# Attention and a routed MoE layer on one core: when queries and keys are loaded, and for how many units at once

## The chip, the core and the metric

One core of one Trainium2 chip runs the whole program in one launch. The metric is the device time of one execution in microseconds (us). The cores' engines are called as the profile calls them: PE (matrix products, with PEld for its weight loads), DVE, ACT and POOL (elementwise work), and SP, which here does nothing but issue DMAs.

## What is computed

For 8 batches and 12 heads, with 448 tokens and a head dimension of 64:

```python
q_n, k_n = (rmsnorm(q, g_q), rmsnorm(k, g_k))
scores = scale * np.matmul(q_n, k_n.transpose(0, 1, 3, 2))
attn = softmax(scores)                       # row maximum taken off, 1e-9 added to the sum
x = np.matmul(attn, v)                       # then as 3584 tokens of 12 * 64 = 768
e_idx = np.argmax(x @ w_gate + modality_bias[modality_id], axis=1)
out[mask] = gate_w[mask, None] * (np.maximum(x[mask] @ w1[e], 0.0) @ w2[e])   # for each of 8 experts
```

All in float32. The products run in PE's fp32r format with a high and a low part of each operand, so that one product takes three passes, or two where parts are stacked.

## The kernel before

**Units and steps.** A unit is two heads of one batch: 48 units. Attention is laid out by hand over steps n, from -22 (`PLAN['start']`) to 335. Unit u's scores are taken in the seven steps 7u to 7u+6, one block of 128 score rows a step (`st`, L974), beside preparatory work for later units and the rest of the work for earlier ones. `plan` says what each step does; `when(what, u)` gives the step, `7u - PLAN[what]`, unless `PLAN['first']` names another for one of the first units. All engines run under a manual schedule, so the order of the program is the order on each engine and on each DMA queue. The routed layer follows from about 580 us on, and the change does not touch it.

**A unit's way.** Its queries and keys are loaded (`load`, the DMA at L794) as [112 partitions, 2 heads, 4 x 64]; squared on ACT (`sumsq`: queries at step 7u-50, keys at 7u-49), summed, turned into a reciprocal root (`rstd`), and scaled on POOL (`norm`, steps 7u-26, queries, then keys). PE transposes them (`tr`, L869: keys at 7u-21, queries at 7u-18), and a step later ACT and DVE split the result into a high and a low part. The parts then have to change partitions, and SP moves them within on-chip memory by DMA (`move`, L882, 112 KB each): in step 7u-20 four moves for the keys (two high, two low), in step 7u-17 four for the queries. The row maximum's products (`sa`, L946) begin at step 7u-14 and read both. `mt` brings the maxima into a row of the queries' tile by a small DMA (L962). Values are loaded at the end of each seventh step (`load_v`, L787), and every third unit's results are stored (`xstore`, L1086).

**The loads' buffers.** There are six slots for queries (`r1[0]`) and six for keys (`r1[1]`), slot u mod 6. A load therefore waits until unit u-6's `norm` has read its slot; a load for two units at once waits for units u-6 and u-5. One `load(u, n, which)` issues one DMA each for queries (0) and keys (1), over n units: 224 KB for one unit, 448 KB for two.

**When they are issued.** Ahead of the steps: units 0 and 1 singly, 2 and 3 together, the gains `g_q` and `g_k`, units 4 and 5 together. At the end of step -12 units 6 and 7 together, keys first. Units 8 and 9 singly at the ends of steps -2 (`7u - PLAN['ld']`, with `ld` 58) and 6. From unit 10 on, for two units at once, keys at the end of step 7u-57 and queries at the end of step 7u-54. Within a step the transposes' moves come first, the loads last.

**SP's queue.** SP issues one DMA after another. Each carries its own wait, so whatever stands behind a waiting DMA waits too.

Of the kernel before, what the change touches and what calls it, by code (L numbers as in the profile page):

```python
# [66 lines left out]
def kernel(  # L67
# [59 lines left out]
    def load_gains():  # L127
        with nc.allow_non_contiguous_dma(reason="gains, one to a partition"):
            for half in range(2):
                SY.dma_start(gg[64 * half : 64 * half + 64, 0:1], g_q.unsqueeze(1))  # L130
                SY.dma_start(gg[64 * half : 64 * half + 64, 1:2], g_k.unsqueeze(1))
# [261 lines left out]
    def view(t, off, p, *dims):  # L393
        n = 1
        for d in dims:
            n *= d
        a = t[:p, off : off + n]
        if len(dims) > 1:
            ax = " ".join("abcd"[: len(dims)])
            a = a.rearrange(f"p ({ax}) -> p {ax}", **dict(zip("abcd"[1:], dims[1:])))  # L400
        return a
# [367 lines left out]
    if True:  # L769
# [19 lines left out]
        def load(u, n=1, which=(0, 1)):  # L789
            b, h0 = u // NP, 2 * (u % NP)  # L790
            for g in which:
                for m in range(n):
                    T.setdefault(u + m, {})["qk"[g]] = ld_b[g][(u + m) % 6]
                SY.dma_start(view(r1[g], QK * (u % 6), CP, 2 * n, NCH * D),  # L794
                             (q, k)[g][b, h0 : h0 + 2 * n].rearrange("h (p c) d -> p h (c d)", p=CP))
# [428 lines left out]

        wps = ps_o.tile([128, 512], F32, tag="o", name="warm")
        A.preload_act_table_set("natural_log_exp_and_others")
        for u, n in ((0, 1), (1, 1), (2, 2)):
            load(u, n)
        load_gains()
        load(4, 2)  # L1230

        pre = {e: {} for e in "AV"}
        post, fin = {}, {}
# [21 lines left out]
        def put(n, *what):  # L1255
            plan.setdefault(n, []).append(what)
# [10 lines left out]
        def xt_at(u):  # L1267
            if u < NU - 8:
                return NJ * (u + 6) + XTJ
            return NJ * (NU - 2 + (u - NU + 8) // 2) + XTE[u % 2]  # L1270

        def when(what, u):
            return P["first"].get((what, u), NJ * u - P[what])

        for u in range(NU):
            for j in range(NJ):
                jj = (0, 1, 2, 4, 5, 6, 3)[j] if u < P["early"] else j
                put(when("sa", u) + j * (P["sastep"] if u == 0 else 1), "sa", u, jj)
            put(when("mt", u), "mt", u)
            if u < NU - 1:  # L1280
                for c in range(4):
                    put(NJ * (u + 1) + (AVJ[c] if u < NU - 2 else min(AVJ[c], 6)), "av", u, c)
            put(xt_at(u), "xt", u)
            if u % 2:
                put(NJ * (u + 1) + (SMJ if u < NP * (B - 2) else P["sml"]), "sums", u - 1)
            if u % 4 == 3:
                put(NJ * (u + 2) + (LAJ if u < NP * (B - 2) else min(LAJ, 4)), "gates", u // 4)
                put(NJ * (u + 2) + (RCJ if u < NP * (B - 2) else min(RCJ, 6)), "recips", u // 4)
            put(when("tk", u), "tr", u, 1)
            put(when("tq", u), "tr", u, 0)  # L1290
            put(when("nq", u), "norm", u, 0)
            put(when("nk", u), "norm", u, 1)
            put(when("sk", u), "sq", u, 1)
            put(when("sq", u), "sq", u, 0)
            if ("rs", u) in P["first"]:
                put(when("rs", u), "rs", u // 3, P["rs0"].get(u, 0), u % 3 + 1)
            elif u > 8 and u % 3 == 2:
                put(when("rs", u), "rs", u // 3, 0, 3)
            if u == 6:
                put(-12, "load", u, 2, (1, 0))  # L1300
            elif u in (8, 9):
                put(when("ld", u), "load", u)
            elif u > 9 and u % 2 == 0:
                put(when("ld", u) + 1, "load", u, 2, (1,))
                put(when("ld", u) + 4, "load", u, 2, (0,))

        for n in range(P["start"], NJ * NU):
            i, j = divmod(n, NJ)
# [127 lines left out]
        u, g = NU - 1, NU // 4 - 1  # L1436
# [182 lines left out]
```

## Time and profile before

| | |
|---|---|
| median of three runs | 1083.87 us (1081.62 to 1086.3) |
| the profiled execution | 1088.99 us |
| its span, first to last instruction | 1087.2 us |
| busy share of the span | PE 96%, DVE 72%, POOL 65%, ACT 64% |
| mean granted clock of PE | 0.986 |
| DMA of the span | 153.72 MB, mean 141 GB/s |

A busy PE means that some product is under way, not that it runs at its peak. The granted clock is the share of PE's full clock, 1.0 (2.4 GHz) or 0.5 (1.2 GHz); a stretch that holds both shows a mean between them. An idle time in brackets in a timeline names what is believed to have ended it.

### The profile page before, as it was taken

The page shows a single profiled execution, that of the slowest core. Times are in us where ns is not written, and L with a number is a line of the kernel's source. Part 1 is how long each engine was busy: PE and PEld are TensorE (multiplying, and loading weights), DVE is VectorE, ACT ScalarE, POOL GpSimd, SP SyncE. Part 2 cuts the span into 40 slices and gives each one's busy share as a digit, 9 for nine tenths or more (in the row PEclk, how much of TensorE's full clock was granted, in tenths as well). Part 3 has the DMA queues.
Part 4 walks back from the last instruction along what each step waited for, and adds up shares of the span by engine and source line. Part 5 has one row for each costly group of instructions (what it writes and reads, how often), then busy time and mean ns, then how long its engine had stood idle before and what let it go on. Part 6 is the DMA issues. An engine that isn't in the chain of part 4 may idle for free.

```text
span 1087.2 us, 18988 instructions
## 1 busy us (share of the span) xinstructions
PE 1047.1 (96%) x6536; PEld 808.6 (74%) x6536; DVE 782.4 (72%) x1351; ACT 696.1 (64%) x1293; POOL 704.7 (65%) x728
## 2 busy tenths in 40 slices
PE   8899999989999999999999999999999999999996
PEld 7645555545555555555556999999999999999995
DVE  5676778968779887798878897667655676566740
ACT  6787888868888787786665555555545555455531
POOL 6787777777876878688776566664455544656451
PEclk9899999989999999999999999999999999999998
DMA  7775767757876669673684822533284422244161
GB/s 177 173 179 123 167 161 170 176 122 163 169 163 165 154 168 165 151 166 90 131 263 132 219 61 78 155 119 93 55 289 147 117 85 67 84 117 117 46 219 61
DMA packets 151704, 153.72 MB, mean 141 GB/s; under 512 B 73434, under 2 KB 141486, under 8 KB 151088
## 3 DMA queue, kind: packets, MB, share of 16 engines
q1 hardware_dynamic: 126244, 110.59, 42.7%
q0 software_dynamic: 25328, 41.82, 12.4%
q8 instruction: 54, 0.88, 0.4%
q14 instruction: 50, 0.41, 0.2%
q10 hardware_dynamic: 28, 0.01, 0.0%
HBM read 150.31 MB, written 33.39 MB: 169 GB/s over the span
## 4 chain that ended last, share of the span: by engine, by line
PE 74%; DMA 8%; DVE 6%; issue 5%; POOL 4%; ACT 2%; SPq 0%; POOLq 0%; DVEq 0%; ACTq 0%
PE ph L565 19%; PE py L595 18%; PE av L1013 11%; PE st L974 11%; DMA w1w<-xw 5%; PE sa L946 4%; PE tr L869 3%; PE xt L1070 2%; DVE at_hlw L52 2%; POOL r2w L52 1%; PE sm L1028 1%; POOL xrw L52 1%; PE warm L1223 1%; ACT xw L52 1%; DVE xw L52 1%
## 5 line engine op out<-in xcount | busy, mean ns | idle before, releaser
L565 PE MATMUL ph<-xw,w1w 128*128 128x256 f32 x2016 | 246.6, 283 | 1.4 <-DVE xw L52 0.8
L565 PEld LDWEIGHTS ph<-xw,w1w 128*128 128x128 f32 x2016 | 244.0, 192 | 3.8 <-issue 1.4
L52 DVE TENSOR_REDUCE at_hlw<-sa 128x1 f32<-128x448 f32 x336 | 205.7, 617 | 42.8 <-PE sa L946 24.4
L974 PE MATMUL st<-w1w 128*128 128x448 f32 (+1 forms) x480 | 177.1, 418 | 0.8 <-DMA w1w<-xw 0.6
L946 PE MATMUL sa<-w1w 128*128 128x448 f32 (+1 forms) x288 | 112.2, 390 | 20.0 <-ACT w1w L52 5.8
L52 POOL TENSOR_TENSOR r2w<-r2w 128x448 f32<-128x448 f32 (+1 forms) x72 | 82.1, 1140 | 64.4 <-DVE r2w L52 23.8
L52 ACT ACTIVATE r2w<-st 128x448 f32<-128x448 f32 x168 | 90.7, 543 | 48.5 <-PE st L974 40.6
L974 PEld LDWEIGHTS st<-w1w 128*128 128x128 f32 (+1 forms) x480 | 85.4, 191 | 45.4 <-ACT r2w L52 15.6
L52 POOL DMA_INDIRECT r<-in_moe_w_dram,tb_w x60 | 78.1, 1301 | 57.8 <-DVE w1w L52 42.5
L595 PE MATMUL py<-w2lw,hhw 128*128 128x384 f32 x448 | 113.7, 334 | 0.0
L52 ACT ACTIVATE hhw<-ph 128x512 fp32r<-128x512 f32 x56 | 33.5, 598 | 120.9 <-PE ph L565 102.0
L52 DVE TENSOR_TENSOR w1w<-r,w1w 128x768 fp32r<-128x768 f32 x112 | 103.4, 953 | 8.9 <-ACT w1w L52 7.3
L52 ACT CAST w1w<-xw 64x448 fp32r<-64x448 f32 x188 | 105.5, 561 | 3.4 <-issue 1.4
L52 POOL DMA_INDIRECT r2w<-in_moe_w_dram,tb_vi x48 | 51.0, 1062 | 86.3 <-DVE w2lw L52 73.7
L52 DVE TENSOR_TENSOR w2lw<-r2w,w2ha 128x1536 fp32r<-128x1536 f32 x28 | 49.1, 1757 | 79.2 <-issue 50.3
L52 ACT ACTIVATE at_w2lw<-st 128x448 f32<-128x448 f32 x168 | 90.5, 544 | 22.6 <-PE st L974 17.5
L974 PE MATMUL st<-w1w,w2ha 65*128 65x448 f32 x288 | 101.1, 371 | 1.1 <-DMA w1w<-xw 1.1
L52 POOL TENSOR_TENSOR xrw<-r,at_hlw 112x512 f32<-112x512 f32 x95 | 98.0, 1051 | 5.0 <-PE tr L869 4.5
L52 ACT CAST w1w<-r 128x768 fp32r<-128x768 f32 x112 | 95.0, 901 | 0.0
L946 PEld LDWEIGHTS sa<-w1w 128*128 128x128 f32 (+1 forms) x288 | 55.8, 194 | 35.1 <-issue 10.5
L52 POOL TENSOR_TENSOR r2w<-r2w,at_w2lw 64x448 f32<-64x448 f32 (+1 forms) x48 | 54.7, 1140 | 41.8 <-DVE r2w L52 18.1
L595 PEld LDWEIGHTS py<-w2lw,hhw 128*128 128x128 f32 x448 | 80.9, 188 | 0.0
(313 smaller groups left out, 2208.5 us busy)
## 6 DMA issues: line engine op xcount, KB each, us to landing
w1w<-xw SPq DMA_DIRECT2D x312, 112.0 KB
xg<-xrw SPq DMA_DIRECT2D x14, 768.0 KB
xrw<-xg SPq DMA_DIRECT2D x56, 192.0 KB
r<-in_q_dram SPq DMA_DIRECT2D x22, 448.0 KB
r<-in_k_dram SPq DMA_DIRECT2D x22, 448.0 KB
w2ha<-xw SPq DMA_DIRECT2D x72, 112.0 KB
r2w<-in_v_dram SPq DMA_DIRECT2D x24, 224.0 KB
at_w2lw<-in_v_dram SPq DMA_DIRECT2D x24, 224.0 KB
```

The source lines that it names most:

```text
L52: return fn(*a, **kw)
L565: PE.matmul(ps[:, i], lhsT=lt_, rhs=rt_[:, c], start=n == 0, stop=n == 17)
L595: PE.matmul(ps[n][:, :384], lhsT=lt_[:, j, 128 * t : 128 * t + 128], rhs=rt_[:, 384 * n : 384 * n + 384], start=j == 0 and m == 0, stop=j ...
L869: PE.transpose(sp[:, c], src[:, c], idn[:CP, :CP])
L946: PE.matmul(ps[:, :S], lhsT=t["qq"][r, h, a : a + 128], rhs=t["kk"][h][r], start=True, stop=True)
L974: PE.matmul(ps[:, :S], lhsT=l, rhs=t["qq"][:, h] if first else t["ql"][:, h], start=first and (j != 3 or h == 0), stop=not first and (j != ...
L1013: PE.matmul(t["av"][64 * h : 64 * h + 64, :S], lhsT=vv[r, u % 3, j], rhs=t["p"][r, j], start=c == 0, stop=c == 3)
L1028: PE.matmul(R[g][32 * i : 32 * i + 32, :S], lhsT=sel[:, m], rhs=T[u + i // 2]["cs"][:, i % 2], start=m == 0, stop=False, tile_position=(0, ...
L1070: PE.transpose(ps[:CP, 128 * c : 128 * c + 128], T[u]["xt"][:, c * CP : (c + 1) * CP], idn)
L1223: PE.matmul(wps[:, :128], lhsT=ones, rhs=idn, start=True, stop=True)
```

## The change

The program's first six units are loaded singly instead of one, one, two and two; so are units 6 and 7, by the plain formula (steps -16 and -9); units 8 and 9 stay as they were. From unit 10 on the loads are still for two units at once. The keys stay at step 7u-57. The queries move from step 7u-54 to step 7u-59, ahead of the keys.

```diff
-        for u, n in ((0, 1), (1, 1), (2, 2)):
-            load(u, n)
+        for u in range(3):
+            load(u)
         load_gains()
-        load(4, 2)
+        for u in range(3, 6):
+            load(u)
...
-            if u == 6:
-                put(-12, "load", u, 2, (1, 0))
-            elif u in (8, 9):
+            if 5 < u < 10:
                 put(when("ld", u), "load", u)
             elif u > 9 and u % 2 == 0:
+                put(when("ld", u) - 1, "load", u, 2, (0,))
                 put(when("ld", u) + 1, "load", u, 2, (1,))
-                put(when("ld", u) + 4, "load", u, 2, (0,))
```

## Rows read from the trace of the kernel before

**Rows 1.** Stretches of four units: us, PE, PEld, DVE, ACT, POOL busy (count), clock, DMA share, GB/s

```profile
134.80:178.60 43.80, 43.80 (x242) 25.47 (x240) 35.98 (x67) 36.18 (x80) 31.86 (x33) 1.00 0.74 178
...
222.80:274.30 51.50, 47.18 (x243) 26.73 (x241) 39.45 (x78) 37.11 (x80) 36.49 (x38) 0.93 0.66 153
...
410.10:458.00 47.90, 45.60 (x243) 26.37 (x241) 35.64 (x67) 36.18 (x80) 35.26 (x36) 0.96 0.81 164
```

**Rows 2.** Waits of PE, 100 to 480 us: total us, times, longest

```profile
PE sa L946 <- issue: 4.7, 2, 4.3
PE sa L946 <- DMA w1w<-xw: 4.3, 4, 2.3
```

**Rows 3.** Timeline of PE: the three longest of these waits (start, us, ...)

```profile
227.95 0.71 PE L946 MATMUL sa<-w1w 128*128 128x448 f32 x1 [4.32 <-issue]
...
320.74 0.44 PE L946 MATMUL sa<-w1w 128*128 128x448 f32 x1 [0.89 <-DMA w1w<-xw]
...
435.42 0.71 PE L946 MATMUL sa<-w1w 128*128 128x448 f32 x1 [2.30 <-DMA w1w<-xw]
```

**Rows 4.** Timeline of SP's queue ahead of the wait at 320 us

```profile
304.10 2.42 SPq L882 DMA_DIRECT2D w1w<-xw  x4
...
307.33 0.60 SPq L794 DMA_DIRECT2D r<-in_k_dram  x1
307.99 1.89 SPq L787 DMA_DIRECT2D r2w<-in_v_dram  x1
310.07 2.61 SPq L882 DMA_DIRECT2D w1w<-xw  x4
...
313.64 0.42 SPq L794 DMA_DIRECT2D r<-in_q_dram  x1
315.16 2.52 SPq L882 DMA_DIRECT2D w1w<-xw  x4
```

**Rows 5.** Chain of waits, two moves: start, us from issue to landing

```profile
34.14 2.02 DMA w1w<-xw
...
315.16 5.45 DMA w1w<-xw
```

**Rows 6.** Timeline of SP's queue and of ACT around the wait at 223 us

```profile
219.63 0.42 SPq L794 DMA_DIRECT2D r<-in_q_dram  x1
220.16 2.44 SPq L882 DMA_DIRECT2D w1w<-xw  x4
...
227.34 0.63 ACT L52 ACTIVATE xrw<-r 112x512 f32<-112x512 f32 x1 [4.67 <-DMA r<-in_q_dram]
```

**Rows 7.** Timeline of PE, of SP and chain of waits at step -5

```profile
30.06 0.71 PE L946 MATMUL sa<-w1w 128*128 128x448 f32 x1 [3.40 <-ACT w1w L52]
...
24.52 2.38 SPq L882 DMA_DIRECT2D w1w<-xw  x4
...
23.94 4.74 DMA r<-in_q_dram
```

**Rows 8.** Stretches of the start, columns as in rows 1

```profile
2.00:12.00 10.00, 10.00 (x78) 9.98 (x76) 3.89 (x11) 4.23 (x9) 6.18 (x13) 1.00 0.97 243
12.00:26.66 14.66, 11.96 (x66) 9.12 (x64) 10.21 (x18) 11.92 (x27) 10.66 (x23) 0.88 0.62 152
26.66:30.06 3.40, 0.00 (x1) 0.03 (x1) 0.00 (x0) 1.79 (x4) 2.25 (x10) 0.87 1.09 241
30.06:34.80 4.74, 4.74 (x19) 4.53 (x20) 2.53 (x5) 1.19 (x4) 2.09 (x3) 0.50 0.89 152
```

**Rows 9.** Timeline of DVE (the gains' product) and of POOL (unit 3's norm)

```profile
11.75 0.16 DVE L52 TENSOR_TENSOR gs<-gg 128x1 f32<-128x1 f32 x1 [1.83 <-DMA gg<-in_g_k_dram]
...
30.18 2.04 POOL L52 TENSOR_TENSOR xrw<-r,at_hlw 112x512 f32<-112x512 f32 x2
```

**Rows 10.** Timeline of SP (a single unit's load) and of POOL (two norms)

```profile
1.73 0.46 SPq L794 DMA_DIRECT2D r<-in_q_dram  x1
...
300.86 2.04 POOL L52 TENSOR_TENSOR xrw<-r,at_hlw 112x512 f32<-112x512 f32 x2
```

## Prediction

> **What bounds the kernel now.** I read the page first, for the engine that is never idle, then the stretches of attention, then what PE waited for, then SP's queue ahead of each such wait. In attention PE is the bound: an undisturbed stretch of four units, 28 steps, took 43.80 us with PE busy for all of them, so a step is 43.80 / 28 = 1.56 us [rows 1]. No load that comes earlier can shorten such a stretch. What the change can win lies in the stretches that took longer: 51.50 us and 47.90 us for the same work [rows 1]. Between 100 and 480 us PE waited 4.7 + 4.3 = 9.0 us for one kind of work alone, the products of the row maxima, `sa` [rows 2], and three waits make most of it: 4.32, 0.89 and 2.30 us [rows 3]. Which `sa` are these? Going by the steps, they are the first of units 19, 27 and 37, at step 7w-14 of an odd unit w, which need the queries that SP moved in step 7w-17.
>
> What is late for them is seen in SP's queue. At 313.64 the queries of units 32 and 33 are loaded, at 315.16 the four moves of unit 27's queries follow [rows 4]; the move that the `sa` waits for landed 5.45 us after its issue, where a move with less ahead of it took 2.02 us [rows 5]. From step 7w-17 to 7w-14 there are three steps, 4.7 us, so 2.02 us fits and 5.45 us does not. A query load of 448 KB (2 units x 2 heads x 448 x 64 x 4 bytes = 459 kB) stands 2 steps ahead of exactly those moves: 7u-54 is 7w-19 with w = u-5. The same order stands at 219.63 and 220.16, and there ACT too waited 4.67 us for that load's data [rows 6]. The mean of 178 GB/s at a DMA share of 0.74 [rows 1] makes some 240 GB/s at full share, so such a load takes the rings 459 / 240 = 1.9 us.
>
> The start has a wait of the same kind. PE stood 3.40 us until 30.06; the row names ACT, but the moves of unit 1's queries were issued at 24.52, right behind the paired loads of units 6 and 7 of step -12, and the chain shows the second of these landing 4.74 us after 23.94 [rows 7]. In that stretch the DMA share is 1.09, full, while it was 0.62 in the stretch before; behind it PE ran 4.74 us at a clock of 0.50 [rows 8].
>
> **The change, part by part.**
>
> *Queries five steps earlier (19 loads).* They now follow the moves of step 7w-17 (w = u-6, even) instead of standing in front of those of an odd unit. Behind them come the keys, the values, and the key moves of step 7w-20, whose reader has six steps, 9.4 us. So the tight moves lose 1.9 us of traffic ahead of them. Lower bound of the gain: each wait shrinks by 1.9 us at most, 0.89 + 1.9 + 1.9, and the small rest of 9.0 - 7.5 = 1.5 goes, 6.2 us together; nothing at all, if the slow landing has another cause than the load. Upper bound: all 9.0 us. I take 7.5, nearer to the upper end, as in the longest case the load itself was the last to land [rows 6]. Then the clock. It was 0.93 over 51.50 us and 0.96 over 47.90 us [rows 1], which is 0.07 x 51.50 + 0.04 x 47.90 = 3.6 + 1.9 = 5.5 us of full clock lost, in stretches that come right behind the two long waits. Bounds 0 and 5.5; I take 3.5, since a remainder of the longest wait may still bring the clock down. Sum: 11 us.
>
> *Units 0 to 5 singly.* The gains' load now has six single loads ahead of it instead of eight units' worth: 2 x 224 KB less, 459 / 243 = 1.9 us at the rate of the start [rows 8]. The product of the gains waited for that load until 11.75 [rows 9], and the keys of unit 0 wait for it. Gain at the first `sa` 0 to 1.9 us. The six extra issues (29 DMAs a tensor instead of 26) cost SP 0.46 us each [rows 10], 2.8 us in all; nothing else is queued on SP between the gains and the first moves, and this is the cover. Without it the first moves would be that much later.
>
> *Units 6 and 7 singly at steps -16 and -9.* The first goes into the stretch with a DMA share of 0.62 [rows 8], ahead of unit 1's key moves; the second goes behind unit 1's query moves instead of ahead of them. So the wait of 3.40 us goes, and with it up to half of the 4.74 us at half clock, 2.4 us. Upper bound of the start with the 1.9: 7.7 us; lower bound 0. What is late next is POOL: it is busy with squares and roots nearly all this time, and unit 3's key norm, the first of the two at 30.18 [rows 9], has to be there for the transpose in step 0, whose products began where the last stretch ends, at 34.80 [rows 8]. POOL itself comes forward only by the 1.9 us, so that norm ends at about 29.3 and step 0 can't begin much before 28.5: at most 6.3 us. I take 5.
>
> *New waits on SP.* The query load now waits for the norm of unit u-5, queued two steps before it on POOL rather than seven. At 300.86 those two norms began and took 2.04 us, while the moves that now stand ahead of the load were issued from 304.10 to 306.52 [rows 4, 10]: 3.6 us to spare, cost 0. For unit 12 alone the plan has that norm (unit 7, step 25) in the same step as the load; SP then stands until it is done, with the values, the keys of step 27 and the moves of step 29 behind it, all wanted steps later: 0. If POOL were later by those 3.6 us all along, it would cost what the second rival says.
>
> *A rule weighed.* At the start, single and paired loads together moved 243 GB/s at a share of 0.97, paired loads alone 241 GB/s at full share [rows 8]; I see no lower rate for the smaller ones, and the sum has none. The Trainium skill (page "DMA: Bandwidth & Descriptors", section "Bandwidth") tells authors to batch DMAs to 1 MiB or more and shows the rate falling with size; by it the single loads would move more slowly and the start would win less or lose. No row here shows that.
>
> **Sum.** 11 + 5 = 16 us of the profiled execution's 1088.99: 1073. That execution is 5.1 us above the median of the runs, and some of the waits above will be what it has more than they; I give them 2 us, and take 14 us from the median of 1083.87: **1070**.
>
> **The rivals.**
>
> 1. *The start gives its gain back.* POOL is in the chain of the first units, and a shorter start may only wait for it. Then the steady 11 us less 2 remain: 1075. For it: the 6.3 us above leave little room. Against: PE's wait at 30.06 was not on POOL. Chance 0.15.
> 2. *Bunching makes the key moves late: slower.* Queries, keys and values, 1120 KB, now come within three steps, ahead of the key moves; POOL's norms, when late, push them closer still. Landing took 5.45 us behind one load [rows 5]; another 1.9 us makes 7.4, and a store of 672 KB (2.9 us) in every third case 10.2, against the 9.4 us of slack. It decides once the moves land over 9.4 us after issue. If they did so by 1.5 us for each of 19 loads, it costs 28 us against a gain of 14: 1098. Against: the queries go 4 steps, 6.2 us, ahead of those moves, three times the 1.9 us that they take. Chance 0.06.
> 3. *The waits are not the load's.* If other traffic or slow stretches of the rings made the moves late, the five steps do nothing: the ACT waits go, PE's stay, and only the start's 5 us or less are won: 1079. For it: a load of 1.9 us doesn't explain 4.32 us. Against: every long wait stands behind such a load. Chance 0.13.
> 4. *Single loads are slower.* If the rings took them at two thirds of the pairs' rate, the first six units' 2.75 MB would take 17 us instead of 11.3, and the start would lose 5 us in place of winning them: 1080. The skill's rule above is of this kind. Chance 0.04.
>
> **How the numbers follow.** The forecast has the remaining 0.62: 1062 to 1077, between all that the bounds allow (9.0 + 5.5 + 7.7 = 22 us) and half of what I take (7 us). The measurement can tell about 0.5%, 5.4 us, from no change. Faster holds the forecast, rival 1 and a third of rival 3's spread: 0.82; the same holds most of rivals 3 and 4: 0.12; slower is rival 2: 0.06. The range reaches from 1060 to 1081, which takes in rivals 1, 3 and 4.
>
> **What would show it.** Right: no wait over 1 us of `sa` on moves between 100 and 480 us, all stretches of four units at 44 to 46 us and a clock of 1.00; no ACT wait on a query load there; the first `st` before 31 us instead of 34.8; query loads directly behind four moves in SP's queue. Wrong: `sa` still waiting at the first step of odd units (rival 3), or now for key moves in even ones (rival 2); PE idle at steps -5 to 5 for POOL's norms (rival 1); ACT waiting for units 2 to 5's loads (rival 4).

## The result and the profile after

The changed kernel takes 1072.62 us in the median of 4 runs (1071.91 to 1073.86), the kernel before, run beside it, 1085.09 (4 runs, 1081.62 to 1087.21): a ratio of 0.9889, 95% interval 0.986 to 0.9919, so it is faster by 0.8 to 1.4%. 1070 had been forecast. The profiled execution took 1072.39 us against 1088.99, its span is 1070.3 us against 1087.2. All of it lies in attention: the last `st` products began at 580.8 us before and begin at 563.5 now.

The stretches of attention first, columns as in rows 1. The first line is the undisturbed stretch, units 9 to 12. The second holds units 13 to 16, the third units 17 to 20, where rows 1 have 51.50 us, and the last units 33 to 36, where rows 1 have 47.90 us.

```profile
131.50:175.20 43.70, 43.70 (x242) 25.41 (x240) 35.88 (x67) 36.89 (x82) 31.90 (x33) 1.00 0.73 180
175.20:219.00 43.80, 43.80 (x239) 25.03 (x238) 38.36 (x80) 36.49 (x82) 34.06 (x39) 1.00 0.69 164
219.00:264.90 45.90, 44.86 (x243) 25.28 (x241) 41.18 (x78) 36.75 (x80) 36.59 (x38) 1.00 0.67 156
399.20:443.00 43.80, 43.80 (x243) 25.50 (x241) 35.30 (x67) 37.00 (x82) 35.28 (x36) 1.00 0.84 177
```

PE is busy nearly all the time now, and its clock, in the last column but two, is 1.00 in each. The reason stands in the view of PE's waits over the same 100 to 480 us as rows 2 (total us, times, longest). This is all that is left of `sa`:

```profile
PE sa L946 <- DVE at_hlw L52: 1.2, 4, 0.4
PE sa L941 <- DVE at_hlw L52: 0.9, 2, 0.4
PE sa L946 <- issue: 0.7, 2, 0.4
```

None is named a move's, and none is over 0.4 us. The two rows that held 9.0 us have become 0.7. What comes late next are short waits on DVE, at most 0.4 us each, 2.1 us together (0.6 of that kind was there before). ACT's wait for query loads in this window was 11.8 us, 6 times; the list of after has no such row. SP's queue shows the new order around the queries of units 32 and 33, which rows 4 have at 313.64 (start, us of issue):

```profile
294.23 2.42 SPq L882 DMA_DIRECT2D w1w<-xw  x4
296.74 0.54 SPq L794 DMA_DIRECT2D r<-in_q_dram  x1
...
298.10 0.57 SPq L794 DMA_DIRECT2D r<-in_k_dram  x1
298.72 2.33 SPq L787 DMA_DIRECT2D r2w<-in_v_dram  x1
301.14 2.92 SPq L882 DMA_DIRECT2D w1w<-xw  x4
```

In rows 4 the load stands 1.5 us ahead of unit 27's four moves of queries. Here it comes directly behind four moves of queries, unit 26's, and the keys and values follow it; the moves of 301.14 are those of unit 27's keys.

The start, in PE's timeline (the first `sa` of units 0 and 1, the first `st` of step 0, the first `sa` of unit 2) and, as the last line, in DVE's for the gains:

```profile
13.04 0.47 PE L946 MATMUL sa<-w1w 64*128 64x448 f32 x1 [0.70 <-ACT w1w L52]
...
26.89 0.45 PE L946 MATMUL sa<-w1w 128*128 128x448 f32 x1
...
29.75 0.45 PE L974 MATMUL st<-w1w 128*128 128x448 f32 x1
...
33.14 0.44 PE L946 MATMUL sa<-w1w 128*128 128x448 f32 x1 [0.32 <-DMA w1w<-xw]
...
9.70 0.68 DVE L52 TENSOR_TENSOR gs<-gg 128x1 f32<-128x1 f32 x1
```

The second line answers to 30.06 in rows 7: it has no bracket, so the wait of 3.40 us is gone. The gains' product begins 2.05 us earlier than in rows 9, the first `sa` 1.53 us earlier (13.04 against 14.57), the first `st` 5.08 us earlier (29.75 against 34.83). Unit 1's first `st` is at 38.4 against 42.8 us: of the 5.1 us, 0.7 are given back inside unit 0.

One thing went the other way. At 90.80 PE waited 1.05 us for POOL:

```profile
90.80 0.87 PE L869 MATMUL tr<-idn,xrw 112*128 112x112 f32 x4 [1.05 <-POOL xrw L52]
...
91.00:94.40 3.40, 3.40 (x11) 1.45 (x9) 1.21 (x2) 2.42 (x6) 3.24 (x4) 0.50 0.24 56
```

The kernel before has the same wait, with the same 1.05 us, and behind it the clock stayed up (the same two views):

```profile
95.13 0.60 PE L869 MATMUL tr<-idn,xrw 112*128 112x112 f32 x4 [1.05 <-POOL xrw L52]
...
95.20:98.60 3.40, 3.40 (x17) 2.02 (x17) 1.65 (x3) 2.77 (x7) 3.24 (x4) 1.00 0.28 63
```

With the clock at 0.50 for 3.4 us after it, 11 products instead of 17 fit into the stretch: 1.7 us lost that this execution of before did not lose. Two later profiles of the changed kernel have the wait too, 1.07 and 1.09 us, and a clock of 1.00 behind it.

### The profile page after: what moved, and what is told of

It reads as the page before. It is cut to its first block, busy times and chain, and to the rows that moved or that the text cites. A ratio compares the mean times of both kernels' runs of the same rounds, so it can differ in the third digit from the quotient of the medians.

```text
span 1070.3 us, 19021 instructions
## 1 busy us (share of the span) xinstructions
PE 1042.9 (97%) x6536; PEld 806.6 (75%) x6536; DVE 783.9 (73%) x1351; ACT 696.7 (65%) x1293; POOL 715.7 (67%) x728
## 3 DMA queue, kind: packets, MB, share of 16 engines
q0 software_dynamic: 25328, 41.82, 12.5%
## 4 chain that ended last, share of the span: by engine, by line
PE 73%; DVE 10%; issue 4%; DMA 4%; POOL 4%; ACT 2%; SPq 1%; POOLq 0%; DVEq 0%; ACTq 0%
PE ph L565 21%; PE py L595 19%; PE av L1013 11%; PE st L974 10%; PE sa L946 4%; DVE at_hlw L52 3%; PE tr L869 3%; DMA w1w<-xw 2%; PE xt L1070 2%; POOL r2w L52 2%; DVE xw L52 1%; PE sm L1028 1%; POOL xrw L52 1%; PE sm L1035 1%; DVE r2w L52 1%
## 5 line engine op out<-in xcount | busy, mean ns | idle before, releaser
L52 ACT ACTIVATE r2w<-st 128x448 f32<-128x448 f32 x168 | 90.8, 544 | 47.8 <-PE st L974 39.7
L52 POOL DMA_INDIRECT r<-in_moe_w_dram,tb_w x60 | 83.1, 1385 | 53.7 <-DVE w1w L52 38.4
L52 ACT ACTIVATE yw<-py,ltn 128x384 f32<-128x384 f32 x55 | 29.4, 580 | 75.3 <-issue 37.0
```

The source lines that it names most:

```text
L52: return fn(*a, **kw)
```

## The experiments

Ten kernels, and the changed kernel twice more, ran in four groups. Those of one group ran on the same chip beside runs of the kernel before, whose median there was 1088.66 to 1092.58 us, so ratios are compared, and microseconds only inside a group. In the first group the diffs are against the kernel before, where nothing else is said; in the others they are against the changed one. In all of them `when("ld", u)` is step 7u - 58.

**The first group takes the change apart.** The queries' place alone:

```diff
+                put(when("ld", u) - 1, "load", u, 2, (0,))
                 put(when("ld", u) + 1, "load", u, 2, (1,))
-                put(when("ld", u) + 4, "load", u, 2, (0,))
```

> Only the query loads from unit 10 on move, from step 7u-54 to 7u-59; the start is that of before. If the parts add up, the first st stays at 34.8 us, the sa waits of PE on moves between 100 and 480 us (9.0 us before) are gone, the clock holds 1.00 there, and the time is 8 to 11 us below before. If the change's gain were the start's alone (rival 3), it is within 2 us of before.

Measured: 1079.34 us (12 runs, 1075.44 to 1082.45), ratio 0.9894 (0.9864 to 0.9924), which is 11.6 us of 1092.58. PE's waits, 100 to 480 us:

```profile
PE sa L946 <- issue: 1.7, 2, 1.4
...
PE sa L946 <- DMA w1w<-xw: 0.5, 1, 0.5
```

9.0 us have become 2.2, with nothing moved but the load, and the stretch of rows 1 that had a clock of 0.93 has 1.00. The start is as before: unit 1 begins at 43.2 us. What follows: with the load out of the way the waits behind it are gone. Of the 2.2 us, 1.4 are one wait at 281.13, the first `sa` of unit 24, whose moves have a store and no load in front of them.

The start alone, with the queries left at 7u - 54 (this one's diff is against the changed kernel):

```diff
-                put(when("ld", u) - 1, "load", u, 2, (0,))
                 put(when("ld", u) + 1, "load", u, 2, (1,))
+                put(when("ld", u) + 4, "load", u, 2, (0,))
```

> Only the single loads of units 0 to 7; the query loads from unit 10 on stay at 7u-54. If the parts add up, the first st comes near 29.8 us, as with the whole change, the sa waits on moves between 100 and 480 us are those of before (some 9 us, a clock under 1.00 in one or two stretches), and the time is 3 to 5 us below before. If the start's gain is given back to POOL later (rival 1), it is within 2 us of before. If the sa waits came of something else that the start shifts, they shrink here too and the time is 8 us or more below before.

Measured: 1084.82 us (12 runs), ratio 0.9951 (0.9916 to 0.9986), 5.4 us. The waits of attention are all there:

```profile
PE sa L946 <- issue: 10.8, 4, 4.6
PE sa L946 <- DMA w1w<-xw: 2.8, 2, 2.2
```

That is 13.6 us, more than the 9.0 of rows 2. The first `st` is at 27.8 us and unit 1 begins at 40.1. As far as the intervals can tell, the two parts add up: 0.9894 x 0.9951 = 0.9846, and the whole change measured 0.9889, 0.9866 and 0.9859 in three groups.

The start's two halves. Only units 6 and 7 singly:

```diff
-            if u == 6:
-                put(-12, "load", u, 2, (1, 0))
-            elif u in (8, 9):
+            if 5 < u < 10:
                 put(when("ld", u), "load", u)
```

> Of the start only units 6 and 7 are loaded singly, at steps -16 and -9; units 0 to 5 and the later queries as before. If the paired loads stand in front of unit 1's query moves, PE's wait of 3.40 us at the first sa of unit 1 goes and the first st comes 3 us earlier, at 31.5 to 32 us; the product of the gains stays at 11.75 us. If the wait came of something else (ACT, as its row names), it stays and the first st is at 34.5 to 35 us.

Measured: 1087.3 us (12 runs), ratio 0.9965 (0.9928 to 1.0001). PE's timeline, the first `sa` of unit 1 and two of unit 0's steps:

```profile
26.86 0.45 PE L946 MATMUL sa<-w1w 128*128 128x448 f32 x1
...
31.57 0.47 PE L946 MATMUL sa<-w1w 128*128 128x448 f32 x1 [1.19 <-DVE at_hlw L52]
...
34.99 0.71 PE L946 MATMUL sa<-w1w 128*128 128x448 f32 x1 [1.53 <-DVE xw L52]
```

The wait of 3.40 us is gone, and the first `st` is at 29.7 instead of 34.83 us. But DVE then kept PE waiting, the clock was 0.50 from 33.9 to 40.7 us, and unit 1 began at 42.3 where before it began at 42.8. The wait was the paired load's; taking it away alone wins 5.1 us, and unit 0 gives all but 0.6 of them back.

Only units 0 to 5 singly:

```diff
-        for u, n in ((0, 1), (1, 1), (2, 2)):
-            load(u, n)
+        for u in range(3):
+            load(u)
         load_gains()
-        load(4, 2)
+        for u in range(3, 6):
+            load(u)
```

> Of the start only units 0 to 5 are loaded singly; units 6 and 7 as a pair at step -12, later queries as before. If the gains' landing sets the first sa, their product comes 1.5 to 2 us earlier (9.7 to 10.3 us instead of 11.75) and so do the first sa and the first paired load; the wait of PE at unit 1's first sa stays at about 3.4 us, and the first st comes 1.5 to 2 us earlier, at 33 us. If single loads are slower (rival 4), ACT waits for units 2 to 5's loads and the first st is at 35 us or later.

Measured: 1085.91 us (12 runs), ratio 0.9963 (0.9929 to 0.9997). DVE's gains and PE at unit 1's first `sa`:

```profile
9.54 0.14 DVE L52 TENSOR_TENSOR gs<-gg 128x1 f32<-128x1 f32 x1
...
28.44 0.71 PE L946 MATMUL sa<-w1w 128*128 128x448 f32 x1 [4.08 <-DMA w1w<-xw]
```

The gains are 2.2 us earlier, the first `st` is 1.6 us earlier (33.2), unit 1's too (41.2), and the wait before unit 1's `sa` is now 4.08 us: it is set by the paired load behind which the moves stand, and a PE that arrives earlier waits longer. This row names the DMA as releaser where rows 7 named ACT. No single load of units 2 to 5 held ACT by more than 0.3 us.

**The second group works on the queries' place**, beside a repeat of the changed kernel.

> The changed kernel once more, so that it shares runs of the kernel before with the three beside it. About 1.1% below before, as first measured; 1.5% if the queries' part and the start's part, measured alone, add up. No sa wait on moves between 100 and 480 us.

Measured: 1073.78 us (6 runs, 1071.0 to 1077.16), ratio 0.9866 (0.9824 to 0.9908). Attention is as in the first profile. The start is not: unit 1 begins at 40.3 us instead of 38.4, since unit 2's first `sa` waited:

```profile
34.16 0.44 PE L946 MATMUL sa<-w1w 128*128 128x448 f32 x1 [2.37 <-DMA w1w<-xw]
```

Is it the queries' place, or is it enough that they don't come between? Here keys and queries change places, the keys taking 7u - 54:

```diff
-                put(when("ld", u) + 1, "load", u, 2, (1,))
+                put(when("ld", u) + 4, "load", u, 2, (1,))
```

> The changed kernel with the two loads exchanged: queries stay at 7u-59, but the keys go to 7u-54, where the queries stood before, so that again 448 KB stand two steps ahead of the odd unit's query moves. Theory (the load delays the moves behind it): PE's sa waits at the first step of odd units come back, 5 to 12 us of them between 100 and 480 us with a clock under 1.00, and the time is 8 to 13 us above the changed kernel, though every query is there in time. If instead the squares on ACT waited for late queries and PE for them, the waits stay away, since the keys are squared a step later than the queries were: time within 3 us of the changed kernel.

Measured: 1082.53 us (12 runs, 1079.39 to 1088.87), ratio 0.9934 (0.9903 to 0.9966): 8.75 us above the changed kernel beside it, whose slowest run is below the fastest of these. PE's waits, 100 to 480 us, then SP's queue and PE at 223 us:

```profile
PE sa L946 <- issue: 8.5, 3, 4.5
PE sa L946 <- DMA w1w<-xw: 0.9, 1, 0.9
...
215.60 0.38 SPq L794 DMA_DIRECT2D r<-in_k_dram  x1
216.07 2.47 SPq L882 DMA_DIRECT2D w1w<-xw  x4
...
223.51 0.71 PE L946 MATMUL sa<-w1w 128*128 128x448 f32 x1 [4.49 <-issue]
```

9.4 us of waits are back, and the load of keys stands where rows 6 have the load of queries. Three waits behind such loads make 7.6 of them; the other, 1.72 us at 281.80, is the one that the queries' place alone left as well. ACT waited for keys too, 4.4 us, but that is not what PE waited for: the first of the four moves of 216.07 landed at 223.42, and PE began at 223.51. It is the place in front of the tight moves that costs, with queries in it or with keys.

A load behind the tight moves as well, but as late as 7u - 52:

```diff
-                put(when("ld", u) - 1, "load", u, 2, (0,))
                 put(when("ld", u) + 1, "load", u, 2, (1,))
+                put(when("ld", u) + 6, "load", u, 2, (0,))
```

> The changed kernel with the queries as late as they can be, at 7u-52: one step's end behind the odd unit's query moves instead of two steps ahead of them, two steps before their squares. Theory: no sa wait of PE on moves, in spite of the late load; ACT waits for nearly every pair's queries, 1 to 3 us each, 20 us or more in all, and PE loses part of that: 3 to 15 us above the changed kernel, with waits on ACT. If the moves' lateness had nothing to do with the load, the sa waits on moves are as before (9 us).

Measured: 1151.49 us (6 runs), ratio 1.0576 (1.0533 to 1.0619), 77.7 us above the changed kernel: a miss by far in size. No `sa` waits on a move any more, as expected, and the load does stand directly behind four moves. But ACT waited 62.1 us for the loads between 100 and 480 us, and PE for ACT. The first list is PE's waits, 100 to 480 us, the next line ACT's longest, then SP's queue and ACT at one such place:

```profile
PE av L1013 <- ACT at_hhw L52: 20.3, 6, 5.5
PE av L1013 <- ACT at_hlw L52: 9.8, 3, 4.8
PE av L1013 <- ACT at_w2hb L52: 9.7, 3, 3.9
...
ACT xrw L52 <- DMA r<-in_q_dram: 62.1, 14, 6.7
...
321.77 3.13 SPq L882 DMA_DIRECT2D w1w<-xw  x4
324.95 0.58 SPq L794 DMA_DIRECT2D r<-in_q_dram  x1
...
329.45 0.63 ACT L52 ACTIVATE xrw<-r 112x512 f32<-112x512 f32 x1 [4.50 <-DMA r<-in_q_dram]
329.99 0.51 ACT L52 COPY at_hhw<-av 128x448 f32<-128x448 f32 x1
```

ACT takes its work in order. The square that waits for the load at 7u - 50 has the copies and exponentials behind it which the next `av` products need (329.99 is one of them), so each late load stops PE too, and the clock falls behind it. The load has a bound on this side as well: it must land before its squares, and two steps, 3.1 us, are not enough for a load that here landed 4.5 us after its issue.

Queries, keys and values closer together, which is the second rival's case:

```diff
-                put(when("ld", u) - 1, "load", u, 2, (0,))
-                put(when("ld", u) + 1, "load", u, 2, (1,))
+                put(when("ld", u) + 2, "load", u, 2, (0, 1))
```

> The changed kernel with queries and keys together at 7u-56, one step ahead of the key moves of step 7u-55, with the values just before: 1120 KB within a step. Rival 2 (the key moves become late): PE waits at the first sa of units for key moves, or SP stands for POOL, and the time is 5 us or more above the changed kernel. Theory (their slack is 9.4 us, the backlog some 4.7 us): no such waits, time within 2 us of the changed kernel.

Measured: 1074.38 us (6 runs, 1072.08 to 1078.81), ratio 0.9869 (0.9827 to 0.9911), the changed kernel's beside it being 0.9866. The waits on moves, 100 to 480 us, as PE has them:

```profile
PE sa L946 <- DMA w1w<-xw: 1.0, 2, 0.7
...
PE st L974 <- DMA w1w<-xw: 0.9, 1, 0.9
```

1.9 us in 380. The place also made SP stand for POOL at its loads, 8.0 us in 6 waits of one row, and the time doesn't show it: the key moves have slack even behind loads that stand closer to them.

**The third group asks what sets the start now.** The gains' load behind two units instead of three:

```diff
-        for u in range(3):
+        for u in range(2):
             load(u)
         load_gains()
-        for u in range(3, 6):
+        for u in range(2, 6):
             load(u)
```

> The changed kernel with the gains loaded behind units 0 and 1 instead of behind units 0 to 2. In the changed kernel ACT waited 1.2 us for the gains' product (9.70 to 10.56 us). If the gains' landing still sets the first sa, their product comes 1 to 2 us earlier and so does the first sa (13.04 us), 1 us; the time falls by 0 to 1.5 us, as far as unit 0 does not give it back. If the norms on POOL set it now, nothing changes.

Measured: 1073.45 us (6 runs), ratio 0.9853 (0.9809 to 0.9897). The gains' product begins 0.42 us earlier than in the changed kernel's first profile, at 9.28, but the first `sa` stands later (PE's timeline, 13.04 there):

```profile
13.52 0.47 PE L946 MATMUL sa<-w1w 64*128 64x448 f32 x1 [1.12 <-ACT w1w L52]
```

So the gains no longer set the first `sa`, and the time cannot be told from the changed kernel's.

Every load from unit 10 on singly, each unit's queries at step 7u - 59 and its keys at 7u - 57:

```diff
-            elif u > 9 and u % 2 == 0:
-                put(when("ld", u) - 1, "load", u, 2, (0,))
-                put(when("ld", u) + 1, "load", u, 2, (1,))
+            elif u > 9:
+                put(when("ld", u) - 1, "load", u, 1, (0,))
+                put(when("ld", u) + 1, "load", u, 1, (1,))
```

> The changed kernel with all loads single: queries of every unit at 7u-59, keys at 7u-57, 112 more bytes-for-bytes equal transfers of 224 KB. What counts by the theory is where a load stands, not its size: no sa wait on moves, 36 more issues of some 0.5 us hidden on SP, time within 2 us of the changed kernel. If smaller loads move at a lower rate (rival 4), ACT or PE wait for them between 100 and 480 us and the time is 4 us or more above the changed kernel. If the paired bursts still cost something, it is 2 us or more below.

The expectation's counts of DMAs were wrong: 38 units in 19 pairs make 2 x 19 = 38 more. Measured: 1077.27 us (6 runs, 1074.55 to 1082.48), ratio 0.9889 (0.9846 to 0.9931). That is 3.8 us above the kernel run beside it, the one with the gains earlier (0.9853), with intervals that overlap: it is no better than pairs, and a small cost is neither shown nor excluded.

**The last group goes after unit 2's wait.** Unit 7's load, which stands ahead of unit 2's moves of queries, goes from step -9 to -1, beside the changed kernel for the third time:

```diff
-('ld', 9): 6,
+('ld', 9): 6, ('ld', 7): -1,
```

> The changed kernel with one load moved: unit 7's from step -9 to step -1, behind unit 2's query moves of step -2 instead of ahead of them. In five of six executions with the changed kernel's start PE waits 1.6 to 3.0 us at unit 2's first sa (step 1), in four of them for those moves. If the load ahead of them delays them, that wait falls under 1 us, unit 1's first st comes 1.5 to 2.5 us earlier (37.5 to 38.5 us instead of a mean of 39.8), and the time is 1 to 3 us below the changed kernel. If the moves are late because ACT casts them late (they are issued right behind it), the wait stays.

> The changed kernel once more, on the same chip as the version beside it: 1.1 to 1.4% below before; a wait of 1 to 3 us at unit 2's first sa in most executions.

Measured: 1072.92 us (5 runs, 1068.96 to 1074.34), ratio 0.9846 (0.9809 to 0.9883), and 1072.68 us (6 runs, 1068.67 to 1079.68), ratio 0.9859 (0.982 to 0.9898): no difference. SP's queue and PE in the changed kernel:

```profile
26.15 0.59 SPq L794 DMA_DIRECT2D r<-in_q_dram  x1
26.79 0.46 SPq L794 DMA_DIRECT2D r<-in_k_dram  x1
27.34 1.10 SPq L882 DMA_DIRECT2D w2ha<-xw  x2
28.55 3.99 SPq L882 DMA_DIRECT2D w1w<-xw  x6
...
33.54 0.56 PE L946 MATMUL sa<-w1w 128*128 128x448 f32 x1 [2.36 <-DMA w1w<-xw]
```

And with unit 7 later:

```profile
32.41 0.44 PE L946 MATMUL sa<-w1w 128*128 128x448 f32 x1 [0.65 <-ACT r2w L52]
...
33.23 0.46 SPq L794 DMA_DIRECT2D r<-in_q_dram  x1
33.73 0.46 SPq L794 DMA_DIRECT2D r<-in_k_dram  x1
...
34.79 7.36 SPq L882 DMA_DIRECT2D w1w<-xw  x8
...
39.82 0.44 PE L974 MATMUL st<-w1w,w2ha 65*128 65x448 f32 x1 [2.03 <-DMA w1w<-xw]
```

The wait of 2.36 us is 0.65 and no longer on a move, and unit 1 begins at 37.3 us instead of 39.7. But the load now stands, with unit 8's, ahead of the next moves: unit 1 took 13.2 us instead of 10.9 and gave all of it back. The DMA that PE waited for until 39.82 is a small one that ACT had issued, at 34.07, and it landed at 39.69, so SP's own DMAs are not the only ones that were late there. It is the steady part's mechanism once more, and in the crowded start this place, too, is in front of something.

## Why the prediction was right

The forecast was the case that came: 1070 against 1072.62, inside the likeliest case's own range. Point by point:

- **Queries five steps earlier** (11 us taken). From unit 1's first `st` to the last of all it is 580.8 - 42.8 = 538.0 us before, 563.5 - 38.4 = 525.1 after, so 12.9 less; the second and third profiles of the changed kernel have 13.3 and 14.2 less, the one with the queries' place alone 11.1, and that kernel's time fell by 11.6 us. The waits went by more than taken: the 9.0 us of rows 2 to 0.7, not 7.5 of 9.0, but 1.5 us of short waits on DVE came in, so the net is near what was taken. The clock came back in full in both long stretches. What it had cost there is 5.1 us, not the 5.5 that the rounded 0.93 and 0.96 give, for it was 0.50 for 6.8 us (227.2 to 234.0) and for 3.4 us (435.4 to 438.8); 1.7 us were lost anew at 91 us. Over all of these 538.0 and 525.1 us, PE's waits fell from 19.5 to 10.9 us, 8.6 less, and the time at a clock of 0.50 from 13.6 to 6.8 us, which is 3.4 us of work. Together that is 12.0 of the 12.9; the other 0.9 is not put down to a row.
- **Why the wait fell by more than the load's 1.9 us.** The prediction had this as a point against itself (third rival), and here a size was off: the load was taken at its 1.9 us on the rings, and what the moves behind it wait for is its landing. The trace keeps the times at which each DMA reports its parts as landed. By the last of them:

  | kernel, issue of the load | load landed after | first move behind it landed at | PE's `sa` began at | its wait |
  |---|---|---|---|---|
  | before, 219.63 | 7.7 us | 227.85 | 227.95 | 4.32 us |
  | before, 313.64 | 6.5 us | 320.61 | 320.74 | 0.89 us |
  | before, 426.69 | 8.3 us | 435.29 | 435.42 | 2.30 us |
  | places swapped, 215.60 | 7.3 us | 223.42 | 223.51 | 4.49 us |
  | places swapped, 354.43 | 7.6 us | 362.46 | 362.56 | 2.26 us |

  Each move landed 0.3 to 0.5 us after the load in front of it (the load was not the last to land, as the prediction had it), and each `sa` began 0.1 us after its move had landed, those whose wait is named "issue" too. Most loads in that place cost nothing. In five profiles (before, the start alone, its two halves, the places swapped) 85 paired loads stood there between 100 and 480 us, and 12 went with a wait of over 1 us. All 12 took 7.2 us or more to land, and beside each of them an indirect DMA of POOL (L1170, which writes the routed layer's lists) was in flight. The 57 loads with none in flight landed in 3.4 to 6.5 us, and no wait behind them was over 0.9 us. So the place decides whether a late landing is felt. That POOL's DMAs make it late is not shown, since no run moves them.
- **The new waits on SP** (0 taken): borne out. The load at 296.74 follows the four moves at once (294.23 + 2.42 = 296.65), and SP's waits for POOL at loads, 100 to 480 us, sum to 4.6 us (2.2 before), none over 0.6.
- **Units 0 to 7 singly** (5 us taken, 0 to 6.3). At the first `st` it is 5.1 us in the profile of after, at unit 1 4.4. Over the eight profiles with exactly the changed start, unit 1 begins at 38.4 to 40.8 us, mean 39.8; with the start of before at 42.8 and 43.2, mean 43.0. So 3.2 us is the better figure, and the 5 was mis-sized by about 2. The wait of 3.40 us was the moves', as the prediction read it, and not ACT's: the first of them landed at 29.97, and PE began at 30.06. (The load in front of them landed at 29.67; the 4.74 us that the prediction took for its landing are only its piece of the chain.) Of the six extra issues put to units 0 to 5, two are those of units 6 and 7, and no part of the sum hung on them. The step that failed is "what is late next is POOL": PE waits 0.7 us for POOL in the start of after, and what comes late instead is unit 2's moves of queries, behind unit 7's single load (up to 3.0 us), and DVE inside unit 0. The gain of each half was also misjudged: units 6 and 7 alone take the 3.40 us away and return nearly all, units 0 to 5 alone lengthen that wait. By unit 1's first `st` the halves win 0.6 and 1.6 us and both together 2.8 against the profile of before; the ratios, 0.9965, 0.9963 and 0.9951, have intervals too wide to add them up.
- **The rule weighed.** At the start the single loads ran at no lower rate: 255 GB/s at a DMA share of 0.93 from 2 to 12 us, where before had 243 at 0.97 [rows 8]. The Trainium skill (page "DMA: Bandwidth & Descriptors", section "Bandwidth") asks for batches of 1 MiB or more, and by it the single loads would have moved more slowly. The trace of the start does not agree for 224 against 448 KB, and with every load single the difference of 3.8 us lies inside the intervals. The 241 GB/s that the prediction took for paired loads alone belong to a stretch with four moves and a load of values as well.
- **The median's step.** 2 of the 16 us were left out because the profiled execution stood above the median. 14 us were forecast, 1085.09 - 1072.62 = 12.5 measured; between the two profiled executions it is 16.6.

The rivals: the first (the start gives its gain back) is true in part, by another cause than POOL; the second (bunching) was tried in a harsher form and cost nothing that can be told, 1.9 us of waits, and in three profiles of the changed kernel no move landed later than 8.3 us after its issue, under the 9.4 of slack; the third (the waits are not the load's) fell, with the queries moved alone and with the places swapped, though the other traffic that it names goes with the late landings; the fourth (single loads slower) was not seen in the start.

No version tried beats the changed kernel by more than the runs can tell.

## What to carry to other kernels

Where big loads and small moves share a queue, list for each move how many steps its reader leaves it, and put the load directly behind the move with the least, not in front of it. Reckon with the load's time from issue to landing at its slowest, not with its bytes over the mean rate. Then look at the load's own reader: if that is an in-order engine with urgent work behind the waiting instruction, a late load costs nearly all of its lateness in the kernel's time. When such a wait is moved, ask what stands behind the load in its new place, since in a crowded stretch the same wait comes up again there.

## What the runs showed of the hardware

- **The moves behind a load landed behind it.** The estimate of a load's own time on the rings was 1.9 us. In front of the five waits of the table the loads landed 6.5 to 8.3 us after their issue, and the moves behind them 0.3 to 0.5 us after the loads.
- **Moves and loads landed late beside POOL's indirect DMAs.** Loads with one in flight took up to 10.1 us to land, those with none at most 6.5 us. In the kernel with the queries' place alone a move with no load in front of it, issued at 274.56, landed at 281.04, 0.3 us after such a DMA of POOL, and PE waited 1.43 us for it. The two go together; which makes which late is not shown.
- **A wait on ACT is passed on nearly whole.** With the queries at 7u - 52 ACT waited 84.2 us for query loads, in 20 waits, of which 62.1 us in 14 waits fall between 100 and 480 us. The kernel took 77.7 us longer, through products that waited and a clock of 0.93 over the 380 us:

```profile
100.00:480.00 380.00, 335.63 (x1709) 189.55 (x1708) 260.63 (x512) 260.27 (x574) 244.08 (x260) 0.93 0.60 138
```

- **The same wait had two outcomes for the clock.** After 1.05 us for POOL it was 0.50 for 3.4 us in the first profile of the changed kernel, and 1.00 in its second and third, after 1.07 and 1.09 us.
- **A row's releaser can be another engine's row.** The wait at unit 1's first `sa` was put down to ACT in rows 7 and to the move in the kernel with units 0 to 5 single, and several waits that went with the load were named "issue", though PE began 0.1 us after a move had landed.
